# Layer 2's down projections of a two-layer FNet/GLU kernel as seven block products instead of eight, with the weights' combinations streamed

## The chip, the cores and the metric

One core of one Trainium2 chip runs the whole kernel. The metric is the device time of one execution in microseconds (us); the times of the kernel before are three runs, of which the median counts. The profile is one profiled execution of the same program; its time is the span from the first to the last instruction.

## The reference

`x` is (1, 2048, 640). Two layers, each made of a Fourier mixing and a gated projection, are applied with the same weights:

```python
x = x + _A_ref(_layernorm(x), dft_seq_re, dft_seq_im, dft_hid_re, dft_hid_im)   # real part of the DFT over rows and columns
x = x + _B_ref(_layernorm(x), w_gate, w_up, w_down)
...
def _B_ref(x, w_gate, w_up, w_down):      # w_gate, w_up: 640 x 1728; w_down: 1728 x 640
    g = jnp.einsum("bsd,df->bsf", x, w_gate)
    u = jnp.einsum("bsd,df->bsf", x, w_up)
    h = _sigmoid(g) * u
    return jnp.einsum("bsf,fd->bsd", h, w_down)
```

## The kernel before, in words

The residual `X` (2048 rows in 16 tiles of 128) stays in SBUF through both layers. The rows are cut into `NB = 4` blocks of 512. Each fp32 operand of a product is held as two fp16 parts, HI and LO, and each product of two operands takes three matmuls (`PASSES`: HI by HI, HI by LO, LO by HI).

**A block in a layer.** First comes the gate-and-up half: the 1728 hidden columns are 13 tiles of 128 (`j` 0 to 12) and a tail of 64 (`j` 13). In block 0 it is the plain product (`gate_up`); in blocks 1 to 3 it is `seven`, which already computes gate and up together as a 2 x 2 x 2 block product with seven products, two tiles `j` and `j+1` at a time. I call one such call a two-tile step; its matmuls (line 1097) have 256 moving columns. In it TensorE runs `part_one` to `part_seven`; ScalarE copies partial sums out of PSUM (`snap`) and applies the sigmoid (`gate`); VectorE adds (`part_three`) and multiplies (`up`); and the result is split into HI (ScalarE) and LO (VectorE) by `up_parts` into the tile `ht`. Then come the downs (`down`, line 1244): for each of the four row tiles of the block and each half (320 columns) of the output, 41 matmuls of 320 moving columns are added in one PSUM bank, and one VectorE operation per half adds the bank to `X` (line 1259). Two banks are in use at a time, out of eight.

**Beside it** the next block is prepared while the downs run: `pair_stats`, `pair_scale`, `pair_apply`, `pair_combine`, `pair_parts` on VectorE, ScalarE and GpSimd, and `pair_transpose`, two DMA transposes for each of two pairs of row tiles, into the buffer `XW` of the next block. Weights are split once in layer 1, written to DRAM, and streamed again for every block (`load_s`: three DMAs, 1 MB for a tile `j`). The down weights (`w 2 j`) are split in layer 1, stay in a fixed region of SBUF (`WDU`), and are loaded once more for layer 2.

**The tests.** The kernel uses symmetries of the DFT matrices, and so it tests that the inputs have them: `load_rows`, `load_cols` and the two `load_hidden_*` fetch pieces of the matrices into one of two rooms, the `test_*` functions compare them on VectorE and `square_rest` sums the squares on ScalarE. `test_w` takes the largest weight of each tile. At the end `test_all` makes a flag; where it is set, `general` would compute everything anew.

**Order.** Everything is written out by hand: `steps` is the order of TensorE's work, and `at(u, f, ...)` puts a job before, or within a two-tile step at quarters of, step `u`. `block[b]` is the first step of block `b`, and `d0` the first step of its downs. Each engine, and SyncE (SP) which issues nearly all DMAs, takes its instructions in the order in which they are written, and waits where an operand is not ready. SBUF places are chosen at build time by `Slots`. PSUM banks are handed out in the order in which they were freed.

Of the kernel before, what the change touches and what calls it, by code (L numbers as in the profile page):

```python
# [13 lines left out]
OP = mybir.AluOpType  # L14
# [33 lines left out]
WMAX = 16.0  # L48
# [22 lines left out]

class Slots:
# [5 lines left out]
    def __init__(self, big):  # L78
        self.big = big
        self.live = {}  # L80
        self.freed = {}
        self.clock = 0
        self.close = False

    def take(self, n, high):
        taken = sorted(self.live.values())
        if self.close:

            ends = [FIX] + [d for _, d in taken]
            free = [(a, b) for a, b in zip(ends, [c for c, _ in taken] + [UNITS]) if a + n <= b]  # L90
            assert free, f"no room for {n}: {taken}"
            if high:
                a = [a for a in range(UNITS - n, FIX - 1, -n) if all(a + n <= c or d <= a for c, d in taken)][:high]
                if a:
                    return self.new(min(a, key=lambda a: max(self.freed.get(u, 0) for u in range(a, a + n))), n)
                a = max(b for _, b in free) - n
            else:
                a = min((a for f in free for a in {f[0], f[1] - n}),
                        key=lambda a: (max(self.freed.get(u, 0) for u in range(a, a + n)), a))
            return self.new(a, n)  # L100
# [13 lines left out]
        return self.new(min(found, key=age), n)  # L114

# [22 lines left out]
PASSES = ((HI, (HI, LO)), (LO, (HI,)))  # L138

# [58 lines left out]
def folded(ctx, tc, pool, dram, big, acc, flag, x, ct, wh, wg, wu, wc, wd, out):  # L198
# [57 lines left out]

    steps = []
# [244 lines left out]

    PARTS = ((256, 640), (640, 1280), (1280, 1664), (1664, 2432))

    def pair_parts(b, i, n):
        v = held["pf", b, i].f32
        h, l = (held["pb", b, i] if n else take(NT, "pb", b, i)).parts
# [565 lines left out]
    def gated_parts(j):  # L1073
        h, s = held["hf", j].f32, take(4, "ht", j, high=True)
        nc.scalar.activation(s.parts[HI], h, AF.Copy)
        nc.vector.tensor_tensor(s.parts[LO], h, s.parts[HI], op=OP.subtract)
        drop("hf", j)
# [24 lines left out]

    def part_one(b, j):
# [3 lines left out]
        v, w = (take(4, n, j, high=6).f32 for n in ("hv", "hw"))  # L1107
# [51 lines left out]
    def up_parts(j):  # L1159
# [3 lines left out]
        v, s = held["hv", j].f32, take(4, "ht", j, high=True)  # L1163
        nc.scalar.activation(s.parts[HI], v, AF.Copy)  # L1164
        nc.vector.tensor_tensor(s.parts[LO], v, s.parts[HI], op=OP.subtract)  # L1165
        drop("hv", j)

    def seven(b, j):
# [14 lines left out]
        def mm(some):  # L1183
# [15 lines left out]
            part_four(b, earlier[1])  # L1199
            for i in js:  # L1200
                part_five(b, i)
# [609 lines left out]
```

## Time and profile before

| what | value |
|---|---|
| median of 3 runs (lowest, highest) | 1163.81 us (1163.38, 1165.28) |
| span of the profiled execution | 1160.1 us |
| TensorE busy in it | 1127.3 us (97%), 8784 matmuls |
| VectorE, ScalarE busy | 737.6 us (64%), 508.2 us (44%) |
| DMA | 216.40 MB, 187 GB/s on average |
| a block's `seven` / its downs, in TensorE's order | about 80.6 us / 44.6 us |
| layer 2: block 0 from 642.5, its downs from 731.4; blocks 1, 2, 3 from 775.9, 901.0, 1026.2 | us from the start of the span |

The page of the profile gives no time for the profiled execution other than its span; the median of the runs lies 3.7 us above it. How to read it: each engine's row has its busy time, the mean duration of one instruction and the idle time before it with what ended it. Where two VectorE instructions follow each other the first one's end overlaps the second one's start a little, so that a sum of mean durations is larger than the busy time of a stretch. A TensorE row's mean duration is longer than the time between two matmuls, since they are pipelined; the busy time divided by the count is the pace.

### The profile page before, as it was taken

Reading aid. Unit: us, or ns where it says so; the run is one execution under the profiler, and the core shown is the slowest. Engines: PE = TensorE matmul, PEld = TensorE weight load, DVE = VectorE, ACT = ScalarE, POOL = GpSimd, SP = SyncE. Lnnn points to the kernel's source line nnn. Section 1 sums busy time; section 2 is a strip of 40 time slices with the busy share of each in tenths; the row PEclk is TensorE's granted clock in tenths of the full one; section 3 lists DMA queues with packets and bytes.
Section 4 is the critical chain, followed back from the end, with each engine's and each line's share of the span. In section 5 each row is a group of like instructions: output and inputs, shape, how many; then the busy total and the mean of one; then the engine's idle time right before and its main releaser. Section 6 shows DMA issues by size and latency. Waiting matters only on the chain.

```text
span 1160.1 us, 22627 instructions
## 1 busy us (share of the span) xinstructions
PE 1127.3 (97%) x8784; PEld 859.6 (74%) x8784; DVE 737.6 (64%) x1636; ACT 508.2 (44%) x1094; POOL 147.6 (13%) x269
## 2 busy tenths in 40 slices
PE   6699999999999999999999999999999999999997
PEld 2467446788878887888776744678887888788874
DVE  7996888768748666685428557747974557525530
ACT  6864575155515653365204312325542555225410
POOL 2312674201002010100000001000100001000000
PEclk9999999999999999999999999999999999999999
DMA  8418698959596977679203552678859682767301
GB/s 278 136 46 242 243 358 267 280 163 234 156 222 185 242 215 187 199 236 261 70 24 108 189 150 81 185 230 251 245 155 252 205 282 93 168 207 246 115 18 38
DMA packets 225621, 216.40 MB, mean 187 GB/s; under 512 B 68034, under 2 KB 181851, under 8 KB 225502
## 3 DMA queue, kind: packets, MB, share of 16 engines
q1 hardware_dynamic: 224862, 212.23, 62.3%
q0 software_dynamic: 640, 2.62, 0.6%
q8 instruction: 71, 1.16, 0.4%
q14 instruction: 48, 0.39, 0.1%
HBM read 171.03 MB, written 30.40 MB: 174 GB/s over the span
## 4 chain that ended last, share of the span: by engine, by line
PE 81%; DMA 3%; POOL 2%; DVE 1%; issue 1%; ACT 1%; SPq 0%; POOLq 0%; DVEq 0%; ACTq 0%
PE acc L1097 36%; PE acc L1244 31%; PE acc L1051 8%; PE acc L855 2%; PE acc L1180 2%; PE acc L773 1%; DMA big<-kept_w 1%; DMA big<-in_ct 1%; POOL big L999 1%; POOL big L1000 1%; DMA kept_s<-big 1%; DVE big L238 0%; POOL big L998 0%; POOL big L1001 0%; DMA big<-kept_s 0%
## 5 line engine op out<-in xcount | busy, mean ns | idle before, releaser
L1097 PE MATMUL acc<-big 128*128 128x256 f16 x4212 | 462.9, 273 | 1.4 <-DVE small L416 1.4
L1097 PEld LDWEIGHTS <-big 128*128 128x128 f16 x4212 | 411.9, 98 | 49.9 <-DMA big<-kept_w 1.7
L1244 PE MATMUL acc<-big 128*128 128x320 f16 x2624 | 357.7, 299 | 0.0
L1244 PEld LDWEIGHTS <-big 128*128 128x128 f16 x2624 | 256.8, 98 | 99.7
L1101 ACT ACTIVATE big<-acc 128x256 f32<-128x256 f32 x312 | 116.1, 381 | 200.1 <-PE acc L1097 198.5
L1051 PE MATMUL acc<-big 128*128 128x512 f16 (+1 forms) x990 | 176.5, 340 | 0.6 <-ACT big L236 0.4
L1051 PEld LDWEIGHTS <-big 128*128 128x128 f16 x990 | 96.5, 98 | 79.6 <-ACT big L236 0.8
L1277 ACT ACTIVATE big<-big 128x768 f32<-128x768 f32 (+8 forms) x104 | 79.4, 764 | 130.4 <-DVE big L1302 94.8
L1165 DVE TENSOR_TENSOR big<-big 128x512 f16<-128x512 f32 x78 | 53.8, 690 | 110.7 <-ACT big L1164 110.7
L1259 DVE SCALAR_TENSOR_TENSOR big<-acc,big 128x320 f32<-128x320 f32 x64 | 28.4, 484 | 88.3 <-PE acc L1244 88.2
L238 DVE SCALAR_TENSOR_TENSOR big<-big 128x640 f16<-128x640 f32 (+6 forms) x81 | 64.5, 834 | 2.8 <-ACT big L236 2.2
L1143 ACT ACTIVATE big<-big 128x512 f32<-128x512 f32 x78 | 47.9, 627 | 39.2 <-DVE big L1134 39.1
L1299 DVE TENSOR_TENSOR big<-big 128x256 f32<-128x256 f32 x64 | 26.6, 416 | 52.6 <-DMA big<-in_ct 51.3
L236 ACT ACTIVATE big<-big 128x640 f16<-128x640 f32 (+7 forms) x81 | 50.7, 665 | 17.0 <-DMA kept_s<-big 7.7
L1134 DVE TENSOR_TENSOR big<-big,acc 128x512 f32<-128x512 f32 x78 | 53.1, 681 | 3.2 <-PE acc L1097 3.0
L1153 DVE SCALAR_TENSOR_TENSOR big<-acc,big 128x256 f32<-128x256 f32 x78 | 32.6, 418 | 33.4 <-PE acc L1097 28.4
L1164 ACT ACTIVATE big<-big 128x512 f16<-128x512 f32 x78 | 48.8, 626 | 7.8 <-DVE big L1155 6.8
L855 PE MATMUL acc<-big 128*128 128x321 f16 (+3 forms) x324 | 49.0, 300 | 1.1 <-DVE big L238 1.1
L855 PEld LDWEIGHTS <-big 128*128 128x128 f16 (+3 forms) x324 | 28.2, 95 | 20.3 <-issue 7.7
L509 ACT ACTIVATE big<-big 128x384 f16<-128x384 f32 (+2 forms) x48 | 28.9, 647 | 31.4 <-DVE big L491 17.6
L1066 DVE SCALAR_TENSOR_TENSOR big<-acc,big 128x512 f32<-128x512 f32 x26 | 17.9, 687 | 35.0 <-PE acc L1051 28.5
L773 PE MATMUL acc<-big 128*128 128x256 f16 (+5 forms) x288 | 36.9, 288 | 2.6 <-DVE big L664 2.6
(183 smaller groups left out, 978.7 us busy)
## 6 DMA issues: line engine op xcount, KB each, us to landing
big<-kept_w SPq DMA_DIRECT2D x125, 320.0 KB
big<-kept_s SPq DMA_DIRECT2D x75, 512.0 KB
big<-in_ct SPq DMA_DIRECT2D x256, 128.0 KB
big<-kept_w SPq DMA_DIRECT2D x78, 192.0 KB
kept_w<-big SPq DMA_DIRECT2D x41, 320.0 KB
big<-in_ct SPq DMA_DIRECT2D x32, 256.0 KB
kept_s<-big SPq DMA_DIRECT2D x13, 512.0 KB
big<-in_wg SPq DMA_DIRECT2D x16, 320.0 KB
```

The costliest lines, as they stand in the source:

```text
L236: nc.scalar.activation(dh, src, AF.Copy, scale=s)
L238: nc.vector.scalar_tensor_tensor(dl, src, s, dh, op0=OP.mult, op1=OP.subtract)
L773: nc.tensor.matmul(o, xv[:, 384 * xp + c0 : 384 * xp + c0 + n], moving(r, cps[cp]), start=(i % 2 == 0 and r == 0 and xp == HI and cp == HI ...
L855: nc.tensor.matmul(ps[:m, :EC], z[:, at : at + m], w[:, 384 * wp : 384 * wp + EC], start=(d == 0 and zp == HI and wp == HI), stop=(d == ND ...
L1051: nc.tensor.matmul(ps, w[wp][:, d * P : (d + 1) * P], xt[:, xp, :], start=(d == 0 and wp == HI and xp == HI), stop=(d == ND - 1 and wp == LO))
L1097: nc.tensor.matmul(ps, wt, xt, start=start and n == 0, stop=n == len(todo) - 1, skip_group_check=not start)
L1101: nc.scalar.activation(dst, ps, AF.Copy)
L1134: nc.vector.tensor_tensor(v, v, other, op=OP.add)
L1164: nc.scalar.activation(s.parts[HI], v, AF.Copy)
L1165: nc.vector.tensor_tensor(s.parts[LO], v, s.parts[HI], op=OP.subtract)
L1244: nc.tensor.matmul(held["pd", e][0][:, :EH], held["ht", j].parts[hp][:, i * P : (i + 1) * P], held["w", 2, j].parts[wp][:, e * EH : (e + 1 ...
L1277: nc.scalar.activation(v, v, AF.Square, accum_out=new_sum()[:p])
```

## The change

**Downs of layer 2.** In layer 2 the 12 full hidden tiles are taken as six pairs (`PAIRS`). A pair, the two halves of the block's rows (256 each) and the two halves of the output columns make a 2 x 2 x 2 block product, and it is computed with seven products. Product `s` runs over all six pairs in one go (`stage`): 6 pairs x 2 row tiles x 3 passes = 36 matmuls. Partial sums stay in PSUM: a bank is added to `X`, and the next product is added into the same bank (`INTO`). Tile 12 and the tail are multiplied as before (`rest_products`, 5 matmuls for each of 8 pieces): three quarters of them at the end of products 1, 5 and 6, the last quarter by itself (`rest_stage`). Order: products 0 and 1 together, rest, products 2 to 6.

**Their left operands.** `pair_sums` makes four more VectorE operations of 128 x 256 for each pair, inside the two-tile step in which the pair is finished (in block 0 after it, `gated_pair`), and `parts_of("hd", "hs", ...)` splits the three new pieces (128 x 768).

**Their right operands.** In layer 1, during the downs of blocks 1 to 3 and the steps just ahead of them, two pairs a block: the raw down weights are loaded (`load_forms`), combined in four VectorE operations of 128 x 320 (`make_forms`), split (`split_forms`) and written to DRAM (`keep_forms`). In layer 2 each product's six pairs (983 KB) are streamed into one of four places in the region `WDU` (`load_stage`), so that `w 2 j` is loaded again for `j` 12 and 13 alone.

**Places and tests.** From block 0 of layer 1 on the SBUF places follow a list written into the file (`PLACES`). In layer 2 `hv` and `hw` of a two-tile step lie in the other block's `XW`, and the next block's split rows in the present one. The largest down weight is tested in layer 1. Layer 2's tests have a third room and are spread over all four blocks: 5 in block 0's gate-and-up half, 13 in each `seven`, 3 in each block's downs, and two later points. The preparation of the next block comes two points later in layer 2, and block 2's row additions go to block 0's gate-and-up half. `WMAX` becomes 4.

```diff
+PAIRS = NF // 2
+FORM = (0, 1, 5, 3, 4, 2, 6)
+STU = PAIRS * EH // UNIT
+DEPTH = 4
...
+    def parts_of(key, to, j, n=4):
+        h, s = held[key, j].f32, take(n, to, j, high=True)
+        nc.scalar.activation(s.parts[HI], h, AF.Copy)
+        nc.vector.tensor_tensor(s.parts[LO], h, s.parts[HI], op=OP.subtract)
+        drop(key, j)
...
+    def pair_sums(key, j, do):
+        a, b = held[key, j].f32, held[key, j + 1].f32
+        a11, a21, a12, a22 = a[:, :HB], a[:, HB:], b[:, :HB], b[:, HB:]
+        if 0 in do:
+            s3 = take(6, "hd", j, high=True).f32[:, HB : 2 * HB]
+            nc.vector.tensor_tensor(s3, a11, a21, op=OP.subtract)
+            nc.vector.tensor_tensor(a21, a21, a22, op=OP.add)
+        if 1 in do:
+            s2, s4 = (held["hd", j].f32[:, k * HB : (k + 1) * HB] for k in (0, 2))
+            nc.vector.tensor_tensor(s2, a21, a11, op=OP.subtract)
+            nc.vector.tensor_tensor(s4, a12, s2, op=OP.subtract)
...
             part_four(b, earlier[1])
+            if pairs:
+                up(earlier[1])
+                sums(earlier[0], (0,))
             for i in js:
                 part_five(b, i)
+            if pairs:
+                sums(earlier[0], (1,))
             up_parts(earlier[0])
-            up(earlier[1])
+            if not pairs:
+                up(earlier[1])
...
             up_parts(earlier[1])
+            sums_parts(earlier[0])
...
+    def make_forms(n):
+        b12, b11, b21, b22 = (held["fr", n].f32[:, k * EH : (k + 1) * EH] for k in range(4))
+        t1, t3, t2, t4 = (held["ft", n].f32[:, k * EH : (k + 1) * EH] for k in range(4))
+        nc.vector.tensor_tensor(t1, b12, b11, op=OP.subtract)
+        nc.vector.tensor_tensor(t3, b22, b12, op=OP.subtract)
+        nc.vector.tensor_tensor(t2, b22, t1, op=OP.subtract)
+        nc.vector.tensor_tensor(t4, b21, t2, op=OP.subtract)
...
+    def load_stage(s):
+        v = fixed(FIX - WDU + STU * (s % DEPTH), STU, "ws", s)
+        nc.sync.dma_start(v.f16, kept["f",][:, FORM[s]].rearrange("p n c -> p (n c)"))
+
+    TAKES = (("ht", 0, 0), ("ht", 1, 0), ("hs", 0, 0), ("ht", 0, 1), ("hs", 0, 1), ("hs", 0, 2), ("ht", 1, 1))
+    INTO = ((0, 0), (1, 0), (0, 1), (2, 3), (0, 3), (2, 1), (0, 2))
+    REST = {1: 0, 5: 1, 6: 2}
...
+    def stage(b, *ss):
...
+                ps, c = held["pd", into, q][0], HB * part + P * q
+                todo = [(n, hp, wp) for n in ns for hp, wps in PASSES for wp in wps]
+                for m, (n, hp, wp) in enumerate(todo):
+                    nc.tensor.matmul(ps[:, :EH], held[key, 2 * n + second].parts[hp][:, c : c + P], w[:, n, wp],
...
+                if s in REST and PAIRS - 1 in ns:
+                    rest_products(ps, q, REST[s], False)
...
+            for s in ss:
+                into, k = INTO[s]
+                for q in range(2):
+                    ps, bk = held["pd", into, q]
+                    add_product(b, q, k, ps)
...
+            if first:
+                for i in range(TB):
+                    for j0, j1 in ((0, 7), (7, NF + 1)):
+                        steps.append(down(b, i, j0, j1, False))
+                continue
+            steps += [stage(b, 0, 1), rest_stage(b), *(stage(b, s) for s in range(2, FORMS))]
+            for s, u in enumerate((-6, -4.5, -3, -1.5, 1, 1.5, 3)):
+                at(d0 + u, load_stage, s)
...
-                u = block[b] - 8 + 1.2 * i
+                u = block[b] - 8 + wait + (1.2 if first else 1.8) * i
...
+        for n in range(PAIRS if first else 0):
+            u = block[1 + n // 2] + 13 + 3.8 * (n % 2)
+            at(u, load_forms, n)
+            at(u + 2, make_forms, n)
+            at(u + 2.2, split_forms, n, 0)
+            at(u + 3.2, keep_forms, n, 0)
+            at(u + 3.5, split_forms, n, 1)
+            at(u + 4.5, keep_forms, n, 1)
...
+                when += [block[0] + 8 + 1.1 * k for k in range(5)] if b == 0 else [block[b] + 2 + 0.9 * k for k in range(13)]
+                when += ([d0 + 4.4 + 0.6 * k for k in range(3)] if b < last else [d0 + 0.9 * k for k in range(3)])
```

In a block's downs of the changed program the order on VectorE is: the four additions of products 0 and 1; `pair_apply`, `pair_combine` and two of the four parts of the next block's first pair of row tiles; the two additions of the rest; the other two parts; `pair_apply` and `pair_combine` of the second pair; the additions of product 2; three parts; the additions of product 3; the last part; then tests and the additions of products 4 to 6. The order on SP is: `load_stage` 4 and 5 (which wait until products 0 and 1 have let go of their places), the first pair's two transposes, `load_s 0`, `load_stage` 6, `load_s 1`, the second pair's two transposes, and then tests, `load_s 2` and `load_s 3`.

More of the change, by code (lines that the diff above doesn't have):

```diff
@@ L82, in __init__ @@
         self.clock = 0
-        self.close = False
+        self.places = None
     def take(self, n, high):
+        if self.places is not None:
+            a = self.places.pop(0)
+            assert all(a + n <= c or d <= a for c, d in self.live.values()), (a, n, self.live)
+            return self.new(a, n)
         taken = sorted(self.live.values())
[L87 to L100, printed above, removed]
         found = []
```

228 lines of the change are left out of this document (167 added, 61 removed), and 21 rows, old and new, of the table PLACES.

## Prediction

> **What bounds the kernel now.** I read the page first, engines and costliest groups.
>
> ```profile
> PE 1127.3 (97%) x8784; PEld 859.6 (74%) x8784; DVE 737.6 (64%) x1636; ACT 508.2 (44%) x1094; POOL 147.6 (13%) x269
> L1244 PE MATMUL acc<-big 128*128 128x320 f16 x2624 | 357.7, 299 | 0.0
> ```
>
> TensorE works 97% of the span, and the downs (line 1244) never wait. So a matmul taken out shortens the span by its pace, as long as nothing else comes late. The chain of waits, in order of time, gives the pace:
>
> ```profile
> 1106.97 44.57 PE acc L1244 x328
> ```
>
> 328 matmuls in 44.57 us are 0.1359 us each. Then the busy time by stretches, cut where TensorE changes between gate-and-up and downs (columns: stretch, length, the five engines' busy time with instruction counts, TensorE clock, DMA share, GB/s):
>
> ```profile
> 96.28:178.30 82.02, 81.41 (x438) 42.40 (x436) 62.87 (x86) 50.88 (x92) 45.36 (x47) 1.00 0.81 282
> 303.40:348.00 44.60, 44.60 (x331) 32.13 (x330) 25.64 (x61) 13.77 (x26) 0.00 (x0) 1.00 0.86 209
> 348.00:430.20 82.20, 80.75 (x741) 72.16 (x739) 58.81 (x150) 45.33 (x107) 11.01 (x30) 1.00 0.79 208
> 775.90:856.50 80.60, 80.60 (x741) 72.22 (x739) 63.79 (x151) 44.04 (x103) 6.32 (x17) 1.00 0.72 215
> 856.50:901.00 44.50, 44.50 (x330) 32.08 (x328) 24.61 (x58) 12.61 (x25) 2.04 (x2) 1.00 0.89 239
> 901.00:981.60 80.60, 80.60 (x740) 72.22 (x739) 49.18 (x123) 43.47 (x101) 4.80 (x16) 1.00 0.60 192
> 1026.20:1106.80 80.60, 80.60 (x739) 72.18 (x738) 38.78 (x78) 39.05 (x101) 0.00 (x0) 1.00 0.55 173
> 1151.40:1160.10 8.70, 0.13 (x1) 0.00 (x0) 0.49 (x1) 0.00 (x0) 0.00 (x0) 0.79 0.07 25
> ```
>
> In layer 2 (775.9 on) TensorE fills every stretch. The two resources that can take its place are VectorE, 79% busy in block 1's `seven`, and the DMA, 89% busy in block 1's downs.
>
> **Part 1, the matmuls.** Per block of layer 2 the downs go from 328 to 7 x 36 + 40 = 292. The built program confirms it: 288 instructions fewer on TensorE, a weight load and a matmul for each of 4 x 36 = 144. Shape and operand types stay, so the pace stays: 144 x 0.1359 = 19.6 us off the path. Downs then take 292 x 0.1359 = 39.7 us.
>
> **Part 2, VectorE in the `seven` stages of layer 2.** The nearest rows for the added operations:
>
> ```profile
> L1133 DVE TENSOR_TENSOR big<-big 128x256 f32<-128x256 f32 x78 | 32.6, 418 | 3.9 <-ACT big L1101 3.8
> L510 DVE TENSOR_TENSOR big<-big 128x768 f16<-128x768 f32 x12 | 11.4, 950 | 0.0
> L229 DVE TENSOR_REDUCE wmax<-big 128x1 f32<-128x640 f16 x40 | 31.1, 805 | 0.0
> L1164 ACT ACTIVATE big<-big 128x512 f16<-128x512 f32 x78 | 48.8, 626 | 7.8 <-DVE big L1155 6.8
> L509 ACT ACTIVATE big<-big 128x768 f16<-128x768 f32 x12 | 10.0, 837 | 2.4 <-DVE big L501 2.4
> 385.48 0.42 DVE L1133 TENSOR_TENSOR big<-big 128x256 f32<-128x256 f32 x1
> 385.82 0.68 DVE L1134 TENSOR_TENSOR big<-big,acc 128x512 f32<-128x512 f32 x1
> ```
>
> The last two rows show that one instruction holds the next up for 0.08 us less than its duration. Per block: 24 sums x (0.418 - 0.08) = 8.1, six LO splits x (0.950 - 0.08) = 5.2. In block 1 the 14 weight tests go (14 x 0.725 = 10.2); 13 DFT tests stay. So 63.8 + 13.3 - 10.2 = 66.9 of 80.6 us, 83%: more than 79%, under TensorE still. Blocks 2 and 3: 62.5 and 52.1, and in block 3 a few tests more. Block 0 goes from 53.1 (next row) to 66.4 and the moved row additions, of 81.1.
>
> ```profile
> 650.30:731.40 81.10, 81.10 (x437) 42.58 (x436) 53.11 (x104) 20.04 (x39) 6.52 (x18) 1.00 0.39 116
> ```
>
> ScalarE gets 6 x 0.837 = 5.0 us on 44: covered. What covers it: a finished pair's pieces are first read by the downs. Pair 10/11 comes last; product 0 and 1 take it only after 60 matmuls (8.2 us), tile 12 after 69 (9.4 us). Cost on the path: not less than nothing (no matmul here waits today), at most rival D. I take 1 us for all three blocks, near nothing because 14 us in the fullest stretch remain.
>
> **Part 3, VectorE in the downs.** This is new: product 2 adds into the bank of product 0, 4 into that of 2, 5 into that of 3, 6 into that of 4. TensorE must wait until VectorE has read the bank, behind whatever is queued there. TensorE's ends, from the downs' start: products 0 and 1 at 11.1, rest 12.5, 2 at 17.4, 3 at 22.3, 4 at 27.2, 5 at 33.4, 6 at 39.7 us. VectorE's queue:
>
> ```profile
> L1259 DVE SCALAR_TENSOR_TENSOR big<-acc,big 128x320 f32<-128x320 f32 x64 | 28.4, 484 | 88.3 <-PE acc L1244 88.2
> L491 DVE TENSOR_SCALAR big<-big,small 128x640 f32<-128x640 f32 x24 | 14.3, 638 | 0.1
> L498 DVE TENSOR_TENSOR big<-big 128x384 f32<-128x384 f32 x12 | 7.1, 591 | 0.4
> L499 DVE TENSOR_TENSOR big<-big 128x256 f32<-128x256 f32 x12 | 5.5, 460 | 0.4
> L501 DVE TENSOR_TENSOR big<-big 128x256 f32<-128x256 f32 x12 | 5.0, 418 | 0.0
> L510 DVE TENSOR_TENSOR big<-big 128x384 f16<-128x384 f32 x24 | 13.2, 551 | 3.8 <-DMA big<-big 3.8
> L510 DVE TENSOR_TENSOR big<-big 128x640 f16<-128x640 f32 x12 | 9.8, 817 | 0.0
> ```
>
> Each less 0.08: the last addition of product 1 ends at 11.6; `pair_apply` 1.1 (12.7); `pair_combine` 1.6 (14.3); two parts 1.2 (15.5); the rest's additions 0.8 (16.3); two parts 1.3 (17.7); the second pair's apply and combine 2.7 (20.3); product 2's additions 0.8: 21.1. Product 4 wants that bank at 22.3: 1.2 us to spare, out of which waits for ScalarE's HI halves come. The others are wide: product 3's additions end at 23.6 and are wanted at 27.2. Price: from nothing to about 2 us a block in blocks 0 to 2 (block 3 prepares nothing). I take 0.3 x 3 = 0.9, because the sum still fits.
>
> **Part 4, the DMA and SP in the downs.** `load_stage` 4 and 5 stand on SP until products 0 and 1 are done, 11.1 us; behind them stand transposes, `load_s` and later tests. The DMA works off its earlier queue meanwhile.
>
> ```profile
> 867.02 5.59 SPq L516 DMA_TRANSPOSE big<-big  x2
> ```
>
> Two transposes take 5.6 us. Large rows run at 282 / 0.81 = 348 GB/s (first stretch above). From 11.1: stages 4 and 5 (1.97 MB) 5.7 us, 16.8; first transposes, ready at 17.7 at the latest and their HI half earlier, 22.4 to 23.3; `load_s 0` (1.05 MB) 3.0, 26.3; stage 6 2.8, 29.1, wanted at 33.4; `load_s 1` 3.0, 32.1; second transposes (inputs ready at 24.5) 5.6, 37.7. The next block wants them at 39.7: 2 us to spare, out of which the landing comes. That is the thinnest cover of the change; before, the second pair was issued 20 us after the downs' start with 24 to go. Price: nothing to 4 us a block; I take 0.5 x 3 = 1.5.
>
> By the Trainium skill (DMA: Bandwidth & Descriptors, Anatomy of one DMA — SWDGE (gpsimd) path) a DMA takes about 2.0 us plus its bytes at 436 GB/s. By it the two transposes (1.1 MB) would take some 4.6 us (an estimate) and the second transposes would have landed at about 32 us instead of 37.7, with the 1.5 us gone. The row above, 5.6 us, speaks against it for transposes, and it stands.
>
> In `seven`, block 1's share 0.72 x 80.6 = 58 us grows by four stages (3.93 MB, 11.3 us) and what spills over; it fits. Loads of tests come late first; the third room gives them 1.8 steps (10 us). The 12 down-weight loads of layer 2 go, in block 0, where they cost nothing.
>
> **Part 5, layer 1.** It is the side that pays without gaining. Rows for combining and splitting:
>
> ```profile
> L920 DVE TENSOR_TENSOR big<-big 128x321 f32<-128x321 f32 x24 | 10.6, 486 | 0.0
> L238 DVE SCALAR_TENSOR_TENSOR big<-big 128x768 f16<-128x768 f32 x13 | 13.4, 1031 | 0.0
> ```
>
> A pair of tiles: 4 x 0.486 + 2240/768 x 1.031 = 4.9 us; two in a block's downs 9.9, and five weight tests 4.0: 25.6 + 13.9 = 39.5 of 44.6 us. Bank use there lets VectorE lag by a whole row tile (11 us). The DMA gets 2 x 1.80 MB, 10.4 us, on 0.86 x 44.6 = 38.4: 48.8 in 44.6, so 4.2 us spill into block 2's `seven` (0.79 x 82.2 = 65 us of work: room). What a late load does there is seen in block 2:
>
> ```profile
> 399.52 0.42 DVE L1299 TENSOR_TENSOR big<-big 128x256 f32<-128x256 f32 x1 [3.04 <-DMA big<-in_ct]
> 400.87 0.42 DVE L1300 TENSOR_TENSOR big<-big 128x256 f32<-128x256 f32 x1 [0.93 <-DMA big<-in_ct]
> 407.25 1.92 PE L1097 MATMUL acc<-big 128*128 128x256 f16 x16 [1.45 <-DVE small L416]
> ```
>
> VectorE stood 4 us for a test's data, and some five us later TensorE stood 1.45 us. Bounds: -1.45 (other places, the stall gone) to +4. I take 0.
>
> **The end** stays: the last addition follows the last matmul, and the output after it; the 8.7 us of the last stretch remain. The indirect output of row tile 2 now starts about 3 us before the last matmul, and is covered.
>
> **Sum.** Span 1160.1 - 19.6 + 1.0 + 0.9 + 1.5 = 1143.9. The median of the runs stands 3.7 us above the span: 1147.6 us.
>
> **Rivals.**
>
> *A, the forecast:* small stalls in blocks 0 to 2. 1145 to 1151; chance 0.55.
>
> *B, all covers hold:* 1160.1 - 19.6 + 3.7 = 1144.2, and 1142.8 if the 1.45 us go too. For it: no wait in layer 2 today at 79% and 89%. Against: margins of 1 to 2 us. Chance 0.20.
>
> *C, the DMA queue becomes the bound at each block's start.* If large loads run in the downs at 239 / 0.89 = 268 GB/s (row 856.50), Part 4's 16.6 us of them become 21.6: the second transposes end at 42.7, 3.0 us late, three times, with the landing up to 4. 1147.6 - 1.5 + 9 to 12: 1155 to 1158. For it: the share in the downs. Against: `load_s` is of large rows. Chance 0.13.
>
> *D, slower: VectorE becomes the bound in `seven`.* Without the overlap (0.08 x 151 = 12.1) block 1 has 63.8 + 12.1 - 11.3 + 15.7 = 80.3 us, and if every split's wait for ScalarE stands open, in six steps 0.63 + 0.63 + 0.84 more: 92.9, 12.3 us over TensorE; block 2 by the same sum 6.7, block 3 nothing. The downs' margin of 1.2 us is then gone too, up to 3.8 us in three blocks. 1147.6 - 3.4 + 19 to 30: 1163 to 1175, 1169 taken. It decides from 1.09 us of stall in each of the 18 two-tile steps that finish a pair. Against it: TensorE can be some 4 us ahead of VectorE, as the stall above shows, and the waits overlap. Chance 0.10.
>
> *E, it does not do what it says,* the flag set by the lower limit and all computed anew, at a multiple: weights of spread 0.4 do not reach 4. Chance 0.02.
>
> Stalls in C are of about 3.4 us. By the Trainium skill (TensorE: Matmul & The Clock Gate, Part 1) an idle window of some 3.4 us halves the clock until as long a busy one has passed; by it C would be about 5 us worse (an estimate). The trace so far does not bear it out:
>
> ```profile
> 35.87 2.50 PE L350 MATMUL twin<-big 128*128 128x320 f32 x4 [7.69 <-ACT big L356]
> 42.00:50.00 8.00, 8.00 (x52) 6.50 (x50) 8.00 (x16) 7.94 (x20) 3.19 (x5) 1.00 0.01 2
> ```
>
> After 7.69 us of idling the clock reads 1.00. It gets no chance of its own.
>
> **How the numbers follow.** The range takes in A, B and most of C, 1143 to 1157. Faster by over 0.2% (2.3 us, about what a measurement of this kernel tells from no change): A, B and C, 0.87 with a rest of D. Within 0.2%: 0.03, the near end of D. Slower: 0.10.
>
> **What would show it.** Right: 1168 matmuls of 320 columns in layer 2 at 0.136 us, block cycles of about 120.5 us. Part 3 wrong: idle time on the down line with VectorE's `add_product` as releaser. Part 4 wrong: idle time ahead of the first matmuls of blocks 1 to 3, released by the transposes, or on the downs, by `kept_f`. Part 2 wrong, and D right: idle time on the `seven` line released by VectorE or ScalarE in blocks 1 and 2. Part 5 wrong: longer stretches from 222.9 to 555.

## The result, and the profile after

| | before | changed |
|---|---|---|
| median (lowest, highest), 4 runs each | 1163.60 us (1162.80, 1165.28) | 1203.61 us (1202.47, 1207.39) |
| span of the profiled execution | 1160.1 us | 1202.8 us |

The ratio is 1.0346, 95% interval 1.0327 to 1.0364: slower by 40 us, where 1147.6 us was forecast. The page of the changed kernel, engines and costliest groups:

```profile
PE 1122.3 (93%) x8640; PEld 849.5 (71%) x8640; DVE 833.8 (69%) x1824; ACT 534.6 (44%) x1130; POOL 149.6 (12%) x269
L1149 PE MATMUL acc<-big 128*128 128x256 f16 x4212 | 476.9, 276 | 46.7 <-DMA big<-kept_w 34.4
L1411 PE MATMUL acc<-big 128*128 128x320 f16 x1008 | 140.8, 299 | 0.0
```

The new downs (line 1411) never wait, as forecast. What waits is the `seven` stage (line 1149): TensorE stood 46.7 us ahead of its matmuls, mostly for streamed weights. The busy time by stretches (stretch, length, five engines' busy time with counts, TensorE clock, DMA share, GB/s), first blocks 1 and 2 of layer 1, then layer 2: the downs of block 0 and the `seven` stages of blocks 1 to 3:

```profile
226.00:315.50 89.50, 83.03 (x740) 72.93 (x740) 65.10 (x155) 40.56 (x99) 8.59 (x26) 0.98 0.70 205
360.05:447.40 87.35, 81.07 (x741) 72.11 (x739) 62.98 (x160) 46.15 (x109) 11.12 (x30) 1.00 0.80 218
750.86:790.50 39.64, 39.64 (x293) 28.57 (x292) 22.71 (x47) 11.40 (x21) 0.00 (x0) 1.00 0.75 195
790.50:884.80 94.30, 83.58 (x740) 72.88 (x738) 69.48 (x171) 47.06 (x110) 7.72 (x18) 0.95 0.91 266
924.50:1020.03 95.53, 84.34 (x741) 73.53 (x739) 64.77 (x161) 49.16 (x111) 7.48 (x18) 0.93 0.84 262
1059.70:1154.84 95.14, 84.85 (x740) 73.63 (x738) 56.31 (x120) 46.61 (x110) 2.25 (x2) 0.95 0.69 232
```

The balance: four downs of layer 2, 39.65 instead of 44.55 us, are -19.6. Three `seven` stages of layer 2 are +43.2 (94.30 + 95.53 + 95.14 against 3 x 80.6); 32 us of that is TensorE standing (length less busy time) and 11 us the same 740 matmuls busy for longer, at a clock below 1. Block 0's downs begin at 750.86 instead of 731.4: layer 1 and the passage are +19.4. With 0.3 less at the end that is the 42.7 us between the spans.

**Where layer 2's stalls come from.** TensorE's timeline (start, length, then in brackets the idle time before and what ended it) in blocks 1 and 3:

```profile
817.07 1.46 PE L1149 MATMUL acc<-big 128*128 128x256 f16 x6 [4.78 <-DMA big<-kept_w]
823.21 36.92 PE L1149 MATMUL acc<-big 128*128 128x256 f16 x324 [4.67 <-DMA big<-kept_w]
1084.62 36.56 PE L1149 MATMUL acc<-big 128*128 128x256 f16 x318 [2.43 <-DMA big<-kept_w]
1129.39 15.80 PE L1149 MATMUL acc<-big 128*128 128x256 f16 x126 [6.29 <-DMA big<-kept_w]
```

The weights are late by some 5 us twice in block 1 (and by 4.15 and 5.29 us in block 2), and by 2.43 and 6.29 us in block 3. SP's timeline ahead of the first stall:

```profile
793.14 6.85 SPq L1496 DMA_DIRECT2D big<-in_ct  x8
800.09 12.85 SPq L409 DMA_DIRECT2D out<-big  x2
813.39 0.33 SPq L1052 DMA_DIRECT2D big<-kept_w  x1
```

Its row in the waits (us in total, times, longest):

```profile
SPq L409 <- DMA out<-big,rows: 36.0, 3, 13.7
```

And GpSimd's timeline:

```profile
804.46 1.31 POOL L405 DMA_INDIRECT out<-big,rows  x1 [71.92 <-DMA out<-big]
809.56 0.96 POOL L405 DMA_INDIRECT out<-big,rows  x1 [3.79 <-DVE big L1122]
```

This is a chain on one DRAM tensor. Row tiles 0 and 3 of a block are stored by SP, 1 and 2 by GpSimd, in the order 0, 1, 2, 3. All four become ready at the end of the new downs (products 5 and 6); in the kernel before they were spread over the 44.6 us of the downs. GpSimd waits until SP's store of tile 0 has landed, and SP's store of tile 3 waits for GpSimd's two. SP stands 12.85 us, and the weights of the next step (line 1052, issued at 813.39) are queued behind it. Block 3's long stall is of another kind. SP's timeline there, then VectorE's row in the waits:

```profile
1090.57 8.75 SPq L1556 DMA_DIRECT2D big<-in_wh  x4
1104.07 9.18 SPq L1556 DMA_DIRECT2D big<-in_wh  x4
```

```profile
DVE big L1560 <- DMA big<-in_wh: 10.6, 3, 4.9
```

The new spread of tests puts all eight of hidden rows (`load_hidden_rows`, two loads each) into block 3's `seven`. SP is held about 9 us by four such loads, VectorE waits for them, and the weights of the last tiles come late. The loads by themselves are not new: the kernel before issued the same 16 of them between 998.6 and 1057.4 us, eight in block 2's downs and eight in block 3's `seven`, and TensorE did not stall there (80.8 us). Here all 16 stand in block 3's `seven`.

**Where layer 1's come from.** TensorE at the starts of blocks 1 and 2, and ScalarE at the second place:

```profile
231.20 54.47 PE L1149 MATMUL acc<-big 128*128 128x256 f16 x480 [3.90 <-DMA big<-kept_w]
366.46 38.15 PE L1149 MATMUL acc<-big 128*128 128x256 f16 x348 [2.97 <-ACT big L1153]
```

```profile
366.02 0.66 ACT L1153 ACTIVATE big<-acc 128x256 f32<-128x256 f32 x2 [2.72 <-DMA kept_f<-big]
```

ScalarE's `snap` may not write its place before the store of a combination (`keep_forms`) has read it. That points at `PLACES`: counted along the program, between its matmuls 700 and 2800 (from block 0's end to block 2 in layer 1), 95 of 206 takes come within 40 matmuls (some 5 us) of the drop of the same place; before it were 46 of 203.

### The profile page after: what moved, and what is told of

It is laid out like the page before. It is cut to its first block, busy times and chain, and to the rows that moved or that the text cites. A ratio compares the mean times of both kernels' runs of the same rounds, so it can differ in the third digit from the quotient of the medians.

```text
span 1202.8 us, 22742 instructions
## 1 busy us (share of the span) xinstructions
PE 1122.3 (93%) x8640; PEld 849.5 (71%) x8640; DVE 833.8 (69%) x1824; ACT 534.6 (44%) x1130; POOL 149.6 (12%) x269
## 5 line engine op out<-in xcount | busy, mean ns | idle before, releaser
L1149 PE MATMUL acc<-big 128*128 128x256 f16 x4212 | 476.9, 276 | 46.7 <-DMA big<-kept_w 34.4
L1149 PEld LDWEIGHTS <-big 128*128 128x128 f16 x4212 | 416.1, 99 | 105.1 <-DMA big<-kept_w 38.9
L1153 ACT ACTIVATE big<-acc 128x256 f32<-128x256 f32 x312 | 113.3, 379 | 187.9 <-PE acc L1149 177.5
L1313 PE MATMUL acc<-big 128*128 128x320 f16 x1312 | 178.9, 299 | 0.0
L1313 PEld LDWEIGHTS <-big 128*128 128x128 f16 x1312 | 128.4, 98 | 49.8
L1081 PEld LDWEIGHTS <-big 128*128 128x128 f16 x990 | 96.3, 98 | 82.3 <-ACT big L262 3.0
L1106 DVE TENSOR_TENSOR big<-big 128x512 f16<-128x512 f32 (+1 forms) x128 | 95.6, 755 | 67.3 <-ACT big L1105 66.4
L1411 PE MATMUL acc<-big 128*128 128x320 f16 x1008 | 140.8, 299 | 0.0
L1411 PEld LDWEIGHTS <-big 128*128 128x128 f16 x1008 | 98.6, 98 | 38.3
L1105 ACT ACTIVATE big<-big 128x512 f16<-128x512 f32 (+1 forms) x128 | 82.3, 664 | 69.0 <-DVE big L1119 44.8
L264 DVE SCALAR_TENSOR_TENSOR big<-big 128x640 f16<-128x640 f32 (+7 forms) x93 | 80.4, 897 | 7.8 <-ACT big L262 7.2
L262 ACT ACTIVATE big<-big 128x640 f16<-128x640 f32 (+8 forms) x93 | 64.1, 724 | 29.7 <-DMA kept_s<-big 9.0
L1502 DVE TENSOR_TENSOR big<-big 128x256 f32<-128x256 f32 x64 | 26.5, 414 | 51.9 <-DMA big<-in_ct 51.8
L1190 DVE TENSOR_TENSOR big<-big 128x256 f32<-128x256 f32 x78 | 32.5, 417 | 18.8 <-ACT big L1153 18.7
```

What stands on the lines that cost most here:

```text
L262: nc.scalar.activation(dh, src, AF.Copy, scale=s)
L264: nc.vector.scalar_tensor_tensor(dl, src, s, dh, op0=OP.mult, op1=OP.subtract)
L1081: nc.tensor.matmul(ps, w[wp][:, d * P : (d + 1) * P], xt[:, xp, :], start=(d == 0 and wp == HI and xp == HI), stop=(d == ND - 1 and wp == LO))
L1149: nc.tensor.matmul(ps, wt, xt, start=start and n == 0, stop=n == len(todo) - 1, skip_group_check=not start)
L1153: nc.scalar.activation(dst, ps, AF.Copy)
L1313: nc.tensor.matmul(held["pd", e][0][:, :EH], held["ht", j].parts[hp][:, i * P : (i + 1) * P], held["w", 2, j].parts[wp][:, e * EH : (e + 1 ...
```

## Experiments

Three causes were on the table: the order of stores on SP, the tests of hidden rows, and the places of layer 1 (with the combinations' own work as the rival). All runs are compared with runs of the kernel before on the same chip. The indented texts were written before each run; where they name runs, e1 is experiment 1, e7 the last run of 5, e9 is 6, and e10 is the first run of 7.

**1. Stores reordered.** In blocks 0 to 2 SP stores tiles 0 and 3, and only then GpSimd 1 and 2.

```diff
-                    if s == 5:
+                    if s == 5 and (final or q == 0):
                         store_x(b, q, slice(0, D))
-                    if s == 6:
+                    if s == 6 and final:
                         store_x(b, q + 2, slice(0, EH if final and q == 1 else D))
+            if FORMS - 1 in ss and not final:
+                for i in (3, 1, 2):
+                    store_x(b, i, slice(0, D))
```

> Blocks 0 to 2 of layer 2 send out their four row tiles in another order: first tile 0 (SP, after product 5), then after product 6 tile 3 (SP), and only then tiles 1 and 2 (GpSimd's indirect stores). Nothing else changes. Theory 1 (SP stands at the store of tile 3 until GpSimd's indirect store of tile 2 has landed, 11 to 15 us in each block's beginning, and the loads of weight tiles 4 and 5 stand behind it): these SP waits go, and with them the stalls of 4.8 and 4.7, 4.2 and 5.3, 2.4 us in blocks 1 to 3 and the slow clock after them; about 25 to 30 us less, 1174 to 1179. Theory 2 (the DMA engines are full, 0.91 busy in block 1, and the loads come late whoever issues them): less than 8 us, 1196 or more.

Measured: 1185.27 us (ratio 1.0169, 1.0120 to 1.0218). SP's timeline at the place shown above, and the stretches of the three `seven` stages:

```profile
806.60 1.02 SPq L409 DMA_DIRECT2D out<-big  x2
807.72 0.40 SPq L1052 DMA_DIRECT2D big<-kept_w  x1
```

```profile
796.50:880.80 84.30, 82.33 (x739) 72.90 (x738) 69.55 (x170) 47.56 (x110) 8.04 (x18) 0.98 1.01 296
920.50:1001.80 81.30, 80.75 (x741) 72.12 (x739) 64.38 (x161) 49.32 (x111) 7.47 (x18) 1.00 0.97 308
1041.50:1134.40 92.90, 83.13 (x740) 72.85 (x739) 57.00 (x123) 45.91 (x110) 2.04 (x2) 0.94 0.71 240
```

The standing of 12.85 us became 1.02; blocks 1 and 2 lost 10.0 and 14.2 us, block 3 only 2.2, where the hidden rows remain. That is 26 us; the span fell by only 20.7 and the median by 18, because layer 1 was 6 us longer in this profile (block 0's downs at 756.8), in stages that the edit does not touch. So layer 1's stalls vary by several us from run to run. The time lies between the two ranges: theory 1 was right on the stalls of blocks 1 and 2, and block 3's are of the other kind.

**2. The same order of stores in the kernel before**, with nothing else touched:

```diff
-            if store:
+            if store and b == NB - 1:
                 store_x(b, i, slice(es[0] * EH, (es[-1] + 1) * EH))
+            elif store and i == TB - 1:
+                for g in range(TB):
+                    store_x(b, g, slice(0, D))
```

> The kernel before, with the stores of blocks 0 to 2 of layer 2 moved to the end of their downs in the changed kernel's order of queues (tile 0 on SP, tiles 1 and 2 on GpSimd, tile 3 on SP); nothing else is touched, no product form, no new transfer. Theory 1 (a store on SP stands until the indirect stores of the same tensor ahead of it have landed, and the next block's weights queue behind it): 8 to 14 us more in each of the seven-product stages of blocks 1 to 3, 1187 to 1206 us, with SP standing 10 us or more at its second store. Rival theory 2 (the stalls of the changed kernel need its new transfers, the 960 KB products, beside the stores): 1162 to 1168 us.

Measured: 1181.19 us (ratio 1.0158, 1.0122 to 1.0194). SP's timeline:

```profile
774.30 11.02 SPq L382 DMA_DIRECT2D out<-big  x2
785.37 6.48 SPq L1296 DMA_DIRECT2D big<-in_ct  x8
791.89 0.60 SPq L1022 DMA_DIRECT2D big<-kept_w  x1
...
1032.26 13.61 SPq L382 DMA_DIRECT2D out<-big  x2
```

SP stands 10 to 14 us in each of the three blocks without any streamed product, so stores bunched in this order are enough for the wait, and theory 2 falls. The price is lower than expected: the stages take 87.2, 83.0 and 89.6 us, 18 us in all. What stands behind the store need not be weights. In block 1 it is the eight loads of tests at 785.37; VectorE waited for them, ScalarE for VectorE, and TensorE stood 3.75 us for ScalarE:

```profile
789.97 0.43 DVE L1302 TENSOR_TENSOR big<-big 128x256 f32<-128x256 f32 x1 [11.93 <-DMA big<-in_ct]
```

In blocks 2 and 3 it stood 1.85 and 6.19 us for weights. That kernel asks for the next block's first weights earlier (8 to 3.5 steps ahead; the changed one 4.5 to 2), which would cover part of it; why the price is lower was not tested.

**3. The combinations' work earlier, and not at all.** First `u = block[1 + n // 2] + 13 + 3 * (n % 2)` instead of `3.8`:

> The second pair of weights' combinations in each of layer 1's blocks comes 0.8 step earlier (13 + 3.0 instead of 13 + 3.8), so that its last write to DRAM is issued 0.8 step, about 4.5 us, before the next block begins. Theory 1 (the stalls of 2.97 and 1.78 us at the beginning of blocks 2 and 3 of layer 1 are ScalarE waiting to overwrite the place from which that write is still reading): both go, about 5 us less, 1198. Theory 2 (these are VectorE being late at the end of the downs, which has as much work as before): no change beyond 1 us.

Measured: 1210.44 us (1.0398, 1.0351 to 1.0445), a miss: the stalls of 2.97 and 1.78 us became 1.91 and 1.98, and nothing was gained. Then without the work (this kernel leaves the combinations out, so that its layer 2 multiplies zeros):

```diff
-            at(u, load_forms, n)
...
-            at(u + 4.5, keep_forms, n, 1)
+        if first:
+            at(block[3] + 13, no_forms)
+            for n in range(PAIRS):
+                for part in range(2):
+                    at(block[3] + 15 + n, write_forms, n, part)
```

> Layer 1 makes no combinations: no raw loads, no VectorE and ScalarE work for them, and the DRAM copy is filled with zeros from a cleared tile in block 3's downs, where the DMA is nearly idle. All SBUF places stay as in the changed kernel, the sections' places included; layer 2's products use zeros for the seven forms. Theory 1 (layer 1's loss of 18.6 us is the work for the combinations): layer 1 gets back nearly all of it, layer 2 begins its gate-and-up at about 652 us instead of 669.8; 1186. Theory 2 (the loss is the SBUF places, which make loads and writes wait for the places' earlier users): blocks 0 and 1 keep their 11 us and only blocks 2 and 3 win about 6; 1197.

Measured: 1197.98 us (1.0281, 1.0240 to 1.0323). Block 0's downs begin at 744.3 instead of 750.9, and the median fell by 5.6, as theory 2 had it: the combinations' work costs some 5 to 6 us, mostly in blocks 2 and 3, where ScalarE's wait for their store is gone with them. Block 1 stays as it was (89.7 us), with the same stall at its start:

```profile
228.71 55.48 PE L1149 MATMUL acc<-big 128*128 128x256 f16 x480 [3.61 <-DMA big<-kept_w]
```

Some thirteen of the nineteen us are something else.

**4. Other places.** The 613 numbers of `PLACES` were worked out anew for the same takes and drops, so that a place rests as long as possible before it is taken again; no other line differs.

> The changed kernel with another list of places alone: the same 613 takes and drops in the same order, but placed so that a place rests longer before it is taken again (in the blocks of layer 1 behind the first, 2 to 10 of about 70 takes per 700 matmuls come within 40 matmuls of the drop before them, where the list of the changed kernel has 31 to 36). Theory 1 (the written-out places make layer 1's loads and snaps wait for readers that have not finished): the stalls at the starts of layer 1's blocks go, layer 1 gives back 10 to 17 of its 19 us, layer 2 keeps its stalls behind the output stores: 1186 to 1195 us. Rival theory 2 (layer 1 is longer because of the combinations' own transfers and instructions, not because of where things lie): 1200 to 1205 us with the same stalls at the blocks' starts.

Measured: 1197.10 us (1190.75 to 1206.21; ratio 1.0297, 1.0230 to 1.0364). Block 1 takes 81.2 us instead of 89.2, block 2 81.5 instead of 87.5, and TensorE's timeline shows the stalls gone at block 1's start and a new one in block 3:

```profile
228.61 70.91 PE L1149 MATMUL acc<-big 128*128 128x256 f16 x648 [0.35 <-DMA big<-kept_w]
...
486.23 4.15 PE L1149 MATMUL acc<-big 128*128 128x256 f16 x23 [3.81 <-ACT big L1153]
```

Block 0's downs begin at 741.3: 9.6 us of the 19.4 came back, just under theory 1's 10 to 17. The median lies outside both ranges, and its interval overlaps that of the changed kernel (1.0327 to 1.0364), so that this run alone does not settle it; the two runs of experiment 5, which differ in the places only, do. Block 3 lost 3.6 us, where ScalarE's `snap` stands behind squares of tests whose data lands late; whether the new places or the spread between runs brought that is open.

**5. Hidden-row tests spread, on top of 1, and all three together.**

```diff
-            tests += [(load_hidden_rows, test_hidden_rows, (r, k)) for r in range(2) for k in range(4)]
+            for r in range(2):
+                for k in range(4):
+                    tests.insert(10 + 5 * (4 * r + k), (load_hidden_rows, test_hidden_rows, (r, k)))
```

> The kernel of e1_stores_reordered with the eight tests of hidden rows spread over the list (one in every five tests, places 10 to 45) instead of standing together in block 3. Theory 1 (the 100-partition loads from the hidden matrix, packed 0.9 of a step apart, hold SP's queue and so the weights of tiles 10 to 12 and VectorE): the seven-product stage of block 3 falls from 92.9 us to 81 to 84, blocks 1 and 2 stay within 2 us of 84.4 and 81.3: 1172 to 1178 us. Rival theory 2 (the queue and VectorE have no room for these loads wherever they stand): block 3 gains, but blocks 1 and 2 lose as much, 1182 to 1188 us.

> All three together: stores reordered, hidden-row tests spread, places repacked. If the three causes are separate and complete, the times add: 1203.6 less 18 to 26 (stores), 10 to 12 (tests) and 10 to 17 (places) gives 1149 to 1166 us, with the seven-product stages of layer 2 at 81 to 84 us and the downs at 39.7 us as in the changed kernel; at the lower end this beats the kernel before (1163.6 us). Rival: the stages that are freed run into the next limit (VectorE's busier blocks, the queue's bytes), then 1166 to 1180 us.

Measured: 1176.13 us (1.0107, 1.0067 to 1.0148) and, with the places, 1165.75 us (1.0006, 0.9979 to 1.0034). In the first the stages of layer 2 took 89.1, 87.0 and 81.1 us where experiment 1 had 84.5, 81.5 and 93.1: block 3 won 12 us, blocks 1 and 2 lost 10. The rival was right on the stages: so packed, the loads cost where they stand. That the time fell into theory 1's range is luck, because layer 1 was shorter by 6 us again. The places alone, between these two runs, are worth 10.4 us, with intervals that do not overlap. The three edits together take back the whole loss, within the range expected, but not as expected: the stages were to take 81 to 84 us, and this is left in layer 2's blocks 1 and 2:

```profile
776.50:868.00 91.50, 85.22 (x741) 73.97 (x739) 68.61 (x165) 48.12 (x111) 7.91 (x18) 0.94 0.91 269
907.60:994.30 86.70, 82.64 (x741) 72.93 (x740) 63.00 (x155) 48.84 (x111) 7.48 (x18) 0.98 0.96 282
```

**6. Hidden tests out of layer 2.** All fourteen go into the last downs of layer 1; layer 2's other 42 stand 1.2 steps apart instead of 0.9; the places are worked out once more.

```diff
+            tests += [(load_hidden_rows, test_hidden_rows, (r, k)) for r in range(2) for k in range(4)]
+            tests += [(load_hidden_cols, test_hidden_cols, (r, j)) for r in range(2) for j in range(3)]
+            when += [u1 + 0.5 + 0.85 * k for k in range(15)]
...
-                ... [block[b] + 2 + 0.9 * k for k in range(13)]
+                ... [block[b] + 2 + 1.2 * k for k in range(10 if b < last else 8)]
```

> e7_stores_tests_places with the fourteen tests of the hidden matrix taken out of layer 2 and put into the last downs of layer 1 (there the transfers keep the engines of the queue busy at 0.35 and VectorE is busy 25 of 54 us); the 42 tests left in layer 2 stand 1.2 steps apart instead of 0.9; the places are packed once more with a longer rest behind stores. Theory 1 (in layer 2 it is the sum of the transfers that is short: DMA share 0.91 and 0.96 in the seven-product stages of blocks 1 and 2, which last 91.6 and 86.8 us): with 5.2 MB and a quarter of the tests less there, all three stages come to 81 to 83 us, the last downs of layer 1 stay at 44.7 us: 1145 to 1154 us, below the kernel before (1164). Rival theory 2 (the loads cost by their form, 100 partitions of 512-byte pieces, wherever they stand): layer 1's last downs or the passage to layer 2 grow by what layer 2 gains, 1160 to 1168 us.

Measured: 1178.45 us (1.0112, 1.0084 to 1.0140), above both ranges. Layer 2 did what theory 1 said: 83.4, 82.3 and 80.7 us. But its reason is not borne out, since the DMA share went up, not down:

```profile
803.20:886.40 83.20, 81.23 (x740) 72.03 (x739) 66.74 (x160) 45.19 (x103) 7.71 (x18) 1.00 0.96 284
```

DMA share times length is 80 us of transfers here and 83 us above, where the stage took 91.5: their sum alone does not explain that length. More likely single late loads stood in front of others in the order of SP and VectorE; for layer 2 this is argued, not shown. In layer 1's last downs, which grew from 44.7 to 69.7 us, one stall shows it; VectorE's timeline, then TensorE's:

```profile
600.97 0.69 DVE L1563 TENSOR_TENSOR big<-big 100x512 f32<-100x512 f32 x1 [8.74 <-DMA big<-in_wh]
```

```profile
605.12 0.43 PE L1313 MATMUL acc<-big 128*128 128x320 f16 x1 [21.86 <-DVE big L264]
```

VectorE waited 9 us for one hidden-row test (and 6.39, 2.04 and 3.07 us for three before it), with the evictions behind it that free TensorE's banks.

**7. Mended.** Six of the row tests behind those evictions, 1.1 steps apart; two in layer 2's downs; the columns in block 3.

> e9_tests_moved_to_layer1 mended: of the hidden tests six (rows) stand in layer 1's last downs, from behind the six evictions of the early sums on and 1.1 steps apart; two rows go into layer 2's downs of blocks 0 and 1, the six of columns into block 3; layer 2's other tests stay 1.2 steps apart, one more in the gate-up. In e9 the tests stood ahead of the evictions in VectorE's order, each waiting for its load, and TensorE stood 21.9 us for a bank. Theory 1 (that order made the stall; the sum of transfers made the stalls of layer 2): no stall over 3 us in layer 1's last downs, seven-product stages of layer 2 at 81 to 85 us as in e9 (83.4, 82.3, 80.7): 1150 to 1157 us. Rival theory 2 (hidden-row loads are late wherever they are): stalls of 5 us or more come back in the last downs of layer 1, the passage or layer 2: 1160 to 1172 us.

Measured: 1161.63 us (0.9980, 0.9962 to 0.9998), in the rival's range, though no stall from layer 1's last downs on is over 2.3 us. The 21.9 us stall is gone, but blocks 1 and 2 of layer 2 took 85.6 and 86.4 us: four tests from 3.4 steps into the downs on pushed the second pair of transposes back. SP's timeline and TensorE's:

```profile
768.62 2.77 SPq L1559 DMA_DIRECT2D big<-in_wh  x2
771.60 8.07 SPq L546 DMA_TRANSPOSE big<-big  x2
```

```profile
781.42 66.56 PE L1149 MATMUL acc<-big 128*128 128x256 f16 x593 [2.21 <-DMA big<-big]
```

These are the late transposes that the prediction's rival C feared, brought here by the order on SP and not by the DMA's rate. So back to three tests, from 4.4 steps on:

```diff
-                ... [block[b] + 2 + 1.2 * k for k in range(10 if b < last else 9)]
+                ... [block[b] + 2 + 1.1 * k for k in range(11 if b < last else 10)]
-                ... [d0 + 3.4 + 0.8 * k for k in range(4)] if b < last
+                ... [d0 + 4.4 + 0.6 * k for k in range(3)] if b < last
```

> e10_tests_split with three tests in each of layer 2's downs again, from 4.4 steps on (behind the second pair of transposes on SP's queue), instead of four from 3.4 steps on; the seven-product stages of blocks 1 to 3 take 11, 11 and 10 tests, 1.1 steps apart. Theory 1 (in e10 the second pair of transposes stood behind the loads of two tests on SP's queue, issued at 771.60 with the block starting at 778.9): the stalls of 2.2 us at the starts of blocks 1 and 2 of layer 2 and the 0.5 to 0.9 us ahead of them go, the other stalls stay: 1154 to 1159 us, seven-product stages of 81 to 84 us. Rival theory 2 (the tests that go back into the seven-product stages cost there what they cost in the downs, since DMA's share is over 0.9 there): 1159 to 1163 us.

Measured: 1155.90 us (1150.96 to 1163.87, 12 runs; ratio 0.9934, 0.9908 to 0.9959), in theory 1's range, 0.7% below the kernel before and well below the changed one. The profiled execution is one of the quicker of the twelve (1152.43 us). Its stretches in layer 2 (downs of block 0, `seven` of blocks 1 and 3) and its costliest group:

```profile
738.80:778.50 39.70, 39.70 (x294) 28.60 (x293) 22.06 (x49) 10.24 (x20) 0.00 (x0) 1.00 0.78 208
778.50:861.10 82.60, 80.70 (x740) 72.19 (x739) 66.81 (x160) 45.69 (x105) 7.65 (x18) 1.00 0.95 290
1022.00:1102.60 80.60, 80.60 (x740) 72.23 (x739) 59.13 (x136) 46.20 (x105) 2.04 (x2) 1.00 0.79 271
```

```profile
L1149 PE MATMUL acc<-big 128*128 128x256 f16 x4212 | 464.1, 273 | 8.9 <-ACT big L1153 5.4 <-DMA big<-kept_w 3.5
```

TensorE stands 8.9 us ahead of the `seven` matmuls instead of 46.7. The stages, from the first to the last matmul in TensorE's timeline (us; these read 0.2 us longer than the cuts above):

| run | layer 1: block 1, 2, 3 | layer 2's first downs at | layer 2: block 1, 2, 3 | span |
|---|---|---|---|---|
| before | 80.7, 82.3, 80.7 | 731.4 | 80.7, 80.7, 80.8 | 1160.1 |
| changed | 89.2, 87.5, 82.8 | 750.9 | 94.5, 95.7, 95.3 | 1202.8 |
| 1 stores | 89.9, 89.5, 83.8 | 756.8 | 84.5, 81.5, 93.1 | 1182.1 |
| 2 the kernel before, stores bunched | 80.9, 80.8, 80.7 | 730.4 | 87.4, 83.2, 89.8 | 1177.2 |
| 3 work earlier | 89.2, 86.1, 84.5 | 749.8 | 96.7, 94.4, 98.3 | 1205.6 |
| 3 without the work | 89.7, 84.2, 81.1 | 744.3 | 92.8, 93.5, 95.9 | 1192.9 |
| 4 places | 81.2, 81.5, 86.4 | 741.3 | 95.0, 93.7, 97.1 | 1193.4 |
| 5 stores, tests | 88.4, 90.0, 83.4 | 751.0 | 89.1, 87.0, 81.1 | 1174.4 |
| 5 all three | 81.4, 83.7, 83.6 | 736.8 | 91.6, 86.8, 80.7 | 1162.3 |
| 6 hidden tests in layer 1 | 82.6, 83.3, 84.6 | 763.5 | 83.4, 82.3, 80.7 | 1176.2 |
| 7 first | 82.9, 84.7, 81.8 | 738.6 | 85.6, 86.4, 81.2 | 1159.9 |
| 7 last | 83.0, 83.4, 82.8 | 738.8 | 82.8, 81.8, 80.7 | 1150.5 |

What stays open: the 7 us that layer 1 still costs in the last kernel, and how much of layer 2's gain in experiment 6 came from taking the hidden rows out and how much from the wider spacing and the new places, since all were changed at once.

## Why the prediction was wrong, point by point

**Part 1 right.** The 292 matmuls of a block's downs take 39.65 us where 39.7 was forecast, 0.1358 us each and none idle: -19.6 us in all, as forecast.

**Part 2 right, rival D did not come.** VectorE is busy 69.5, 64.8 and 56.3 us (66.9, 62.5 and 52.1 plus a few tests forecast), and of the 46.7 us ahead of the `seven` matmuls VectorE ended two long waits, 2.64 us in layer 1 (line 1503, a test) and 1.75 us in block 2 of layer 2 (line 442).

**Part 3 right.** No idle time on the new downs; the margin of 1.2 us held.

**Part 4 is the step that failed.** Its sum for the transposes came out, in part by luck: the second pair was done 35.9 us after the downs' start where 37.7 was reckoned, but it began at 24.7 instead of 32.1 and held SP 11.1 us instead of 5.6. No block of the changed kernel begins late for it.

```profile
775.61 11.11 SPq L546 DMA_TRANSPOSE big<-big  x2
```

But the queue that it wrote out was not SP's whole queue. The output stores of the same stage were left out, so that their waits were put at nothing without a reason; and the sum stopped at the block's start, while the stores come up on SP some 10 us after it. The whole part was put at 1.5 us; the stores alone cost some 26 us (experiment 1, the slow clock behind the stalls included), and experiment 2 shows the wait without the rest of the change. The other 12 us in block 3 belong to its last sentences: the third room with its 10 us was to cover late tests. For hidden rows packed into one stage it did not.

**Part 5 failed by its size.** Taken at 0 with an upper bound of 4, it measured 19.4. The sum of instructions and bytes was made; that the places were reused sooner was taken as a chance for gain ("other places, the stall gone"). The list of places was in the program and could have been counted. About 5 to 6 us are the combinations' work (experiment 3) and about 10 the places (experiments 4 and 5); with the spread between runs of layer 1 the two are not exact, and some 4 us are left without a cause.

**The clock rule** was dismissed on the clock column of a row of the opening. That was wrong for the stages, and for the row itself too (last section). The slow clock adds 11 us in layer 2 and 2.4 in layer 1's block 1 (busy time over 80.6).

**The range** ended at 1157, and either the stores or layer 1 alone would have carried the time beyond it. The one slower rival, D, took VectorE's work as the danger; that did not come. None asked which instruction the change made to stand at the head of a queue.

## What to carry to other kernels

When a change concentrates work that was spread out, list everything that was issued inside it, the output stores too, and follow each queue past the stage's end to the next weight load; a wait at the head of that queue costs whatever is behind it. Stores of one DRAM tensor from two queues should be ordered so that the queue which also loads weights goes first. Where SBUF places are fixed by hand, count how soon each is taken again: a layer can slow down without one instruction more on its path.

## What the runs showed of the hardware

TensorE's clock can fall after a stall in the middle of the kernel. The rows are from the changed kernel: behind stalls of 2.97 us, of 4.78 and 4.67 us, and of 2.43 us (the third last column is the granted clock):

```profile
366.50:368.50 2.00, 2.00 (x19) 1.79 (x19) 1.96 (x6) 1.10 (x4) 0.00 (x0) 1.00 0.26 77
817.00:820.00 3.00, 1.46 (x6) 0.74 (x6) 0.00 (x0) 0.38 (x1) 0.00 (x0) 0.50 1.05 295
823.20:825.20 2.00, 1.99 (x10) 1.44 (x11) 2.00 (x6) 0.49 (x2) 0.00 (x0) 0.50 1.21 251
827.20:829.20 2.00, 2.00 (x21) 1.79 (x20) 0.73 (x3) 0.15 (x1) 0.00 (x0) 1.00 0.84 224
1086.00:1088.00 2.00, 2.00 (x11) 1.44 (x10) 1.29 (x3) 1.31 (x3) 0.00 (x0) 0.50 0.33 99
```

After 2.97 us the clock is whole. After 4.78 us it is a half, six matmuls take 1.46 us, and behind the second stall it is whole again by 827.2, 4 us after the work went on. The 11 us that layer 2's matmuls are busy for longer go with six such stalls, some 2 us for each on top of itself. The length of a stall does not decide alone: after the 2.43 us ahead of 1084.62 the clock was at a half within 2 us. The Trainium skill (TensorE: Matmul & The Clock Gate, Part 1) gives an idle window of about 3.4 us and as long a busy one. The return after 4 us and the stalls of over 4 us agree with it; the stall of 2.43 us is shorter than that window.

The opening, from which the prediction concluded otherwise, is no counterexample. The clock column reads 1.00 there, but the matmuls of 128x256 were as slow as at half the clock. The first row is of the kernel before from 42 to 46 us, the second of the changed one from 823.2 to 825.2, where the column reads 0.50; at the whole clock the mean is 273 ns:

```profile
L773 PE MATMUL acc<-big 128*128 128x256 f16 x14 | 3.4, 419 | 2.4 <-DVE big L664 2.4
L1149 PE MATMUL acc<-big 128*128 128x256 f16 x10 | 2.3, 418 | 4.7 <-DMA big<-kept_w 4.7
```

So where the column matters, it has to be checked against the durations of the same form.

Issuing a load of hidden rows (200 KB) takes SP 1.36 us in the median of 16 in the changed kernel and up to 3.55, a load of sequence rows (128 KB) 0.60 us in the median of 256; the 8.75 us for four shown above hold waits beside. In the kernel before the same 16 loads of hidden rows took 0.81 us in the median, so their form alone does not set it. By the Trainium skill (DMA: Bandwidth & Descriptors, Why a DMA increments its semaphore by 16 and not by 1) a DMA uses the largest number of engines, up to 16, that divides the slowest dimension on both sides; for these loads (5 and 100) that would be five of sixteen (worked out from the page). No run here shows the engines singly, and another form of the load was not tried.
